# Two padding tiles change size: where the right-hand operands of TensorE start, modulo 512 bytes

## The chip, the cores and the metric

One core of one Trainium2 chip. The time is the device time of one execution in microseconds, the median of the runs shown; less is better. The profile was taken on one execution of the same program.

## What is computed

Attention through 32 pooled tokens per head, then two MLPs, all in float32 (only the sizes that matter are shown):

```
q, k, v: (8, 8, 576, 64)   p: (8, 8, 32, 64)
p_packed = softmax(p @ k.T / 8) @ v
a        = softmax(q @ p_packed.T / 8) @ p_packed      # -> x: (4608, 512)
x = (silu(x @ w_gate) * (x @ w_val)) @ w_out           # 512 -> 1536 -> 512
h = x @ w_in                                           # 512 -> 2048
return (h * cos(h)) @ w_out2                           # 2048 -> 512
```

## The kernel before, in words

Every large product is made with numbers split in two parts (`hi` and `lo`, type float32r): a product takes three matmuls, named by PASSES (hi·hi, hi·lo, lo·hi). Three of the four large products are, besides, done by a seven-product Strassen scheme; its seven products ("pieces") are numbered 0 to 6 and come in the order ORDER = 0, 4, 6, 1, 2, 3, 5. All work is issued in an order written out by hand, engine by engine; pools of tiles sit on the left or the right side of SBUF, and a pool's place is fixed by what is open on its side.

The stages, with their TensorE lines:

- **First MLP, gate and value products with attention** (L535, and L495 for their weights): per batch and per 128 hidden columns, matmuls of 288 moving columns. Moving operand `a2`, stationary operand `wp`, both in the pool `ups` on the right.
- **First down projection** (L652, function `strassen`): five sets of tokens, four with 512 moving columns per matmul and one, the fourth, with 256. Seven pieces of 36 matmuls in each set. Moving operand `g` (pools `da`, `db`, on the left), stationary operand `w1`. The tiles of `w1` lie on the left for pieces 0, 3 and 5 and on the right, in the pool `gates`, for pieces 4, 6, 1 and 2:

```
575     W1_AT = {0: ("da", 3), 3: ("db", 6), 5: ("db", 6)}
...
583             both = late["gates"].tile([128, 2, 2, 512], F32R, tag="w", name="w1", bufs=6)
...
652                         PE.matmul(
653                             out=acc[:, m, :N], lhsT=wd1[n, fp][:, j, 256 * x + 128 * m:256 * x + 128 * m + 128],
654                             rhs=g1[n, fp][:, y, j, :],
```

- **Second MLP, up projection** (L971, function `product`): 2016 matmuls of 384 columns, moving operand `xs`, stationary operand `up`:

```
971                 PE.matmul(
972                     out=out, lhsT=w[:, u, 128 * k:128 * k + 128], rhs=x[:, v, k, :],
```

- **Second MLP, down projection** (L1056, function `down_mm`): 2016 matmuls of 384 columns, moving operand `xs` (new tiles of the same pool), stationary operand `wd`.

`up` and `wd` lie on the left. `xs` has a pool of its own on the right, opened once `gates` and `pad` are closed, near the end of the first down projection. ScalarE and VectorE write `xs` and `g` in a helper (L111, L112).

Two tiles are never read or written; they only shift what comes after them on the right side: `right_pad` in the pool `pad` (opened first, so that it shifts `gates` and `ups`) and `late_pad` in the pool of `xs`:

```
101     ident = pad.tile([128, 128], F32, name="ident")
102     zero = pad.tile([128, 128], F32, name="zero")
103     pt = [pad.tile([128, NPAIR, NP], F32, name=f"pt{i}") for i in range(2)]
104     pad.tile([128, 8], F32, name="right_pad")
...
900                     late["x"] = ctx.enter_context(tc.tile_pool(name="xs", bufs=1, side="right", reuse_waits="tile"))
901                     x_now = [new_xs() for _ in range(7)]
902                     late["x"].tile([128, 8], F32, name="late_pad")
```

Of the kernel before, what the change touches and what calls it, by code (L numbers as in the profile page):

```python
# [10 lines left out]
F32 = mybir.dt.float32  # L11
# [55 lines left out]
def attention_mlp_kernel(ctx: ExitStack, tc: tile.TileContext, qT, kT, vP, pP, wgv, w12, out):  # L67
# [6 lines left out]
    def pool(n, side=None):  # L74
        kw = {"side": side} if side else {}
        return stage[n].enter_context(tc.tile_pool(name=n, bufs=1, reuse_waits="tile", **kw))

    pad = pool("pad", "right")
# [22 lines left out]
    ident = pad.tile([128, 128], F32, name="ident")  # L101
    zero = pad.tile([128, 128], F32, name="zero")
    pt = [pad.tile([128, NPAIR, NP], F32, name=f"pt{i}") for i in range(2)]
    pad.tile([128, 8], F32, name="right_pad")
    half_pi = cst.tile([128, 1], F32, name="half_pi")
    quarter = cst.tile([128, 1], F32, name="quarter")
    warm = cst.tile([128, 1], F32, name="warm")
# [348 lines left out]
    def w2_flush():  # L456
        while w2_dve:
            w2_dve.pop(0)()

    def w2_step():  # L460
        w2_flush()
        if w2_todo:
            w2_dve.append(w2_todo.pop(0)())
# [133 lines left out]
    def load_h(s_, k, t):  # L597
        if s_ < len(SETS):
            t0, N = SETS[s_]
            for fp in range(3):  # L600
                r = raw1[s_, k, t, fp] = hr_tile((k, t), [128, 2, N], "hr")
                f0 = NP1 * k + 2 * fp
                SP.dma_start(out=r, in_=h1[f0:f0 + 2, :, t0 + N * t:t0 + N * t + N].rearrange("f p n -> p f n"))
# [10 lines left out]
    def prep(s_, n, fp):  # L614
        if s_ >= len(SETS):
            return
        N = SETS[s_][1]
        k, t = {0: (0, 0), 4: (1, 0), 6: (1, 1), 1: (1, 1), 3: (0, 1), 2: (0, 0), 5: (1, 0)}[n]
        g = g1[n, fp] = g_first.pop() if g_first else new_g(N)
        split(raw1[s_, k, t, fp], g[:, 0], g[:, 1])  # L620

    def sums1(s_, i):
        todo = {
            1: [((0, 1), (0, 1), (0, 0), fp) for fp in range(3)],
            2: [((1, 1), (1, 1), (0, 1), fp) for fp in range(3)],
            3: [((0, 0), (1, 1), (0, 0), fp) for fp in range(3)],
            4: [((1, 0), (1, 0), (1, 1), 0)],
            5: [((1, 0), (1, 0), (1, 1), fp) for fp in (1, 2)],
        }
        for to, x, y, fp in todo.get(i, ()):  # L630
            to, x, y = (raw1[s_, k, t, fp] for k, t in (to, x, y))
            DVE.tensor_tensor(out=to, in0=x, in1=y, op=ALU.subtract)
# [55 lines left out]
    late = {}  # L688
# [16 lines left out]
    def load_x2(c):  # L705
        for a in range(2):
            for t in range(2):
                xb[a, t] = xt([128, 2, TH], F32, "xb")
                r0 = 2 * TH * c + TH * t
                SP.dma_start(out=xb[a, t], in_=x2d[2 * a:2 * a + 2, :, r0:r0 + TH].rearrange("k p n -> p k n"))  # L710
# [7 lines left out]
    def sums_x2(n):  # L718
        sum_x2(*(("t1", (0, 1), (0, 0)), ("t2", (1, 1), "t1"), ("t3", (1, 1), (0, 1)), ("t4", (1, 0), "t2"))[n])
        if n == 2:  # L720
            del xb[0, 1]

    def new_xs():
        return late["x"].tile([128, 2, 2, TH], F32R, tag="xs", name="xs", bufs=9)

    def split_x2(n, to):
        if to[n] is None:
            to[n] = new_xs()
        split(xb.pop(RIGHT[n]), to[n][:, 0], to[n][:, 1])

    with tc.manual_schedule():
# [142 lines left out]
        def nxt(s_, i):  # L874
            return (s_, ORDER[i + 1]) if i < 6 else (s_ + 1, ORDER[0])

        for s_ in range(len(SETS)):
            end = s_ == len(SETS) - 1
            for i in range(7):
                evict = strassen(s_, i)  # L880
                sums1(s_, i)
                for fp in range(3):
                    prep(*nxt(s_, i), fp)
                if i == 4:
                    load_h(s_ + 1, 0, 0)
                elif i == 5:
                    load_h(s_ + 1, 1, 1)
                    load_h(s_ + 1, 0, 1)
                elif i == 6:
                    load_h(s_ + 1, 1, 0)  # L890
                for _ in range(STEPS_D[s_][i]):
                    w2_step()
                if (s_, i) == (3, 6):
                    w2_flush()
                if end and i == 1:
                    load_x2(0)
                elif end and i == 4:
                    stage["gates"].close()
                    stage["pad"].close()
                    late["x"] = ctx.enter_context(tc.tile_pool(name="xs", bufs=1, side="right", reuse_waits="tile"))  # L900
                    x_now = [new_xs() for _ in range(7)]
                    late["x"].tile([128, 8], F32, name="late_pad")
                    for n in range(3):
                        sums_x2(n)
                elif end and i == 5:
                    sums_x2(3)
                elif end and i == 6:
                    for n in range(7):
                        split_x2(n, x_now)
                evict()  # L910
# [396 lines left out]
```

## Time and profile before

| | us |
|---|---|
| runs | 1423.08, 1420.67, 1418.03 |
| median | 1420.67 |
| the profiled execution | 1422.05 |
| its span in the profile | 1420.3 |

The profiled execution has 1.7 us outside its span and is 1.4 us above the median. The profile's times are microseconds of the span; a group of instructions has a count, a busy time and the mean length of one. Matmuls are pipelined: one starts before the last has ended, so the length of a matmul (393 ns, say) is not what it costs. What it costs is the distance from its start to the next one's start. The timeline gives a merged group of matmuls with its start, its length from the first start to the last end, and its count; the distance is (length less one matmul's length) divided by (count less one). All distances below are worked out so.

### The profile page before, as it was taken

The page shows a single profiled execution, that of the slowest core. Times are in us where ns is not written, and L with a number is a line of the kernel's source. Part 1 is how long each engine was busy: PE and PEld are TensorE (multiplying, and loading weights), DVE is VectorE, ACT ScalarE, POOL GpSimd, SP SyncE. Part 2 cuts the span into 40 slices and gives each one's busy share as a digit, 9 for nine tenths or more (in the row PEclk, how much of TensorE's full clock was granted, in tenths as well). Part 3 has the DMA queues.
Part 4 walks back from the last instruction along what each step waited for, and adds up shares of the span by engine and source line. Part 5 has one row for each costly group of instructions (what it writes and reads, how often), then busy time and mean ns, then how long its engine had stood idle before and what let it go on. Part 6 is the DMA issues. An engine that isn't in the chain of part 4 may idle for free.

```text
span 1420.3 us, 25277 instructions
## 1 busy us (share of the span) xinstructions
PE 1400.6 (99%) x9644; PEld 1286.9 (91%) x9644; DVE 1132.3 (80%) x1515; ACT 829.2 (58%) x1226; POOL 258.6 (18%) x424
## 2 busy tenths in 40 slices
PE   8999999999999999999999999999999999999998
PEld 6678888888898888897899999999999999999998
DVE  6779889888857898997768778787778778787785
ACT  5856666656645555553567777686775444444442
POOL 1112222222220111121011111121211202112020
PEclk9999999999999999999999999999999999999999
DMA  8947978786898746556584233242897765747641
GB/s 343 408 164 275 352 273 301 286 320 249 290 365 315 262 153 245 183 198 242 194 343 155 111 147 144 112 149 108 290 382 243 270 203 188 245 134 262 209 130 34
DMA packets 148504, 329.35 MB, mean 232 GB/s; under 512 B 21664, under 2 KB 58016, under 8 KB 146976
## 3 DMA queue, kind: packets, MB, share of 16 engines
q1 hardware_dynamic: 111040, 202.15, 40.7%
q0 software_dynamic: 36480, 123.76, 22.4%
q10 hardware_dynamic: 864, 1.84, 0.4%
q8 instruction: 76, 1.25, 0.4%
q14 instruction: 44, 0.36, 0.1%
HBM read 202.38 MB, written 125.30 MB: 231 GB/s over the span
## 4 chain that ended last, share of the span: by engine, by line
PE 73%; issue 13%; DVE 5%; DMA 4%; POOL 3%; ACT 2%; SPq 0%; POOLq 0%; DVEq 0%; ACTq 0%
PE o L652 16%; PE o L1056 15%; PE pv L535 7%; PE pg L535 7%; PE ac L971 7%; PE pb L1056 4%; PE pd L1056 4%; PE pd L971 3%; POOL h L991 2%; PE wp L495 2%; PE pb L971 2%; PE pv L524 2%; PE pg L524 1%; DMA hr<-h 1%; PE pp L234 1%
## 5 line engine op out<-in xcount | busy, mean ns | idle before, releaser
L652 PE MATMUL o<-g,w 128*128 128x512 f32 (+1 forms) x1260 | 263.6, 371 | 3.5 <-DVE g L112 1.8
L652 PEld LDWEIGHTS o<-g,w 128*128 128x128 f32 x1260 | 218.8, 188 | 47.9 <-DVE g L112 2.8
L1056 PE MATMUL o<-xs,wd 128*128 128x384 f32 x1440 | 254.3, 336 | 0.5 <-DVE xs L112 0.5
L1056 PEld LDWEIGHTS o<-xs,wd 128*128 128x128 f32 x1440 | 251.9, 187 | 0.9 <-DVE xs L112 0.9
L971 PE MATMUL ac<-xs,up 128*128 128x384 f32 x1152 | 219.5, 338 | 0.6 <-ACT v L1008 0.6
L971 PEld LDWEIGHTS ac<-xs,up 128*128 128x128 f32 x1152 | 204.5, 187 | 1.0 <-ACT v L1008 0.9
L112 DVE TENSOR_TENSOR xs<-raw,xs 128x768 fp32r<-128x768 f32 x168 | 149.6, 950 | 36.1 <-ACT xs L111 36.1
L111 ACT ACTIVATE xs<-raw 128x768 fp32r<-128x768 f32 x168 | 132.4, 843 | 73.1 <-DVE raw L1095 70.8
L111 ACT ACTIVATE g<-hr 128x1024 fp32r<-128x1024 f32 (+1 forms) x105 | 101.1, 975 | 91.8 <-PE o L652 42.3
L535 PE MATMUL pv<-a,wp 128*128 128x288 f32 x1008 | 150.6, 298 | 2.9 <-DVE h L567 2.8
L535 PEld LDWEIGHTS pg<-a,wp 128*128 128x128 f32 x1008 | 137.7, 188 | 16.8 <-issue 5.7
L535 PE MATMUL pg<-a,wp 128*128 128x288 f32 x1008 | 150.3, 298 | 0.5 <-ACT E L208 0.5
L535 PEld LDWEIGHTS pv<-a,wp 128*128 128x128 f32 x1008 | 137.6, 188 | 11.5 <-DVE h L567 5.7
L112 DVE TENSOR_TENSOR g<-hr,g 128x1024 fp32r<-128x1024 f32 (+1 forms) x105 | 113.1, 1113 | 35.5 <-ACT g L111 35.2
L553 ACT ACTIVATE silu<-pg 128x576 f32<-128x576 f32 x96 | 62.4, 651 | 112.8 <-PE pg L535 103.9
L971 PE MATMUL pd<-xs,up 128*128 128x384 f32 x576 | 117.2, 338 | 0.0
L567 DVE TENSOR_TENSOR h<-silu,pv 128x576 f32<-128x576 f32 x96 | 72.1, 751 | 52.2 <-PE pv L535 17.2
L971 PEld LDWEIGHTS pd<-xs,up 128*128 128x128 f32 x576 | 102.8, 187 | 0.0
L568 POOL DMA_DIRECT2D h<-h x96 | 53.4, 556 | 243.6 <-DVE h L567 221.7
L1105 POOL DMA_DIRECT2D out<-ot x80 | 49.5, 622 | 243.7 <-DVE ot L1100 181.5
L1095 DVE TENSOR_TENSOR raw<-raw,raw 128x768 f32<-128x768 f32 x96 | 85.3, 948 | 3.0 <-DMA raw<-h 3.0
L1011 DVE TENSOR_TENSOR hs<-v,pd 128x384 f32<-128x384 f32 x96 | 53.0, 552 | 33.7 <-PE pd L971 29.7
(130 smaller groups left out, 2065.6 us busy)
## 6 DMA issues: line engine op xcount, KB each, us to landing
raw<-h SPq DMA_DIRECT2D x96, 384.0 KB, 7.6
wd<-w2d SPq DMA_DIRECT2D x136, 256.0 KB, 4.0
h<-h POOLq DMA_DIRECT2D x96, 288.0 KB, 5.4
hr<-h SPq DMA_DIRECT2D x48, 512.0 KB, 7.5
raw<-in_w SPq DMA_DIRECT2D x44, 512.0 KB, 5.0
h<-cp POOLq DMA_DIRECT2D x48, 384.0 KB, 2.9
h<-cs POOLq DMA_DIRECT2D x48, 384.0 KB, 2.8
up<-w2u SPq DMA_DIRECT2D x56, 256.0 KB, 6.4
```

The costliest lines, as they stand in the source:

```text
L111: ACT.activation(out=hi, in_=src, func=AF.Copy)
L112: eng.tensor_tensor(out=lo, in0=src, in1=hi.bitcast(F32), op=ALU.subtract)
L535: PE.matmul(out=p_[:, c, :HS], lhsT=w[:, u, x, o:o + 128], rhs=a2[b][:, u, y, HS * c:HS * c + HS], start=(n == 0), stop=(n == 5),)
L553: ACT.activation(out=s_, in_=pg[:, :, :HS], func=AF.Silu)
L567: DVE.tensor_tensor(out=h_, in0=s_, in1=pv[:, :, :HS], op=ALU.mult)
L568: nc.gpsimd.dma_start(out=h1[f, :, S * b:S * b + S], in_=h_.rearrange("p c n -> p (c n)"))
L652: PE.matmul(out=acc[:, m, :N], lhsT=wd1[n, fp][:, j, 256 * x + 128 * m:256 * x + 128 * m + 128], rhs=g1[n, fp][:, y, j, :], start=(first a ...
L971: PE.matmul(out=out, lhsT=w[:, u, 128 * k:128 * k + 128], rhs=x[:, v, k, :], start=(first and k == 0 and i == 0), stop=(k == 1 and i == 2) ...
L1011: DVE.tensor_tensor(out=out, in0=x, in1=y, op=ALU.add)
L1056: PE.matmul(out=acc[m], lhsT=wd[n, 2 * fp + j][:, x, 128 * m:128 * m + 128], rhs=g2[n, fp][:, y, j, :], start=(first and fp + j + q == 0), ...
L1095: DVE.tensor_tensor(out=to, in0=x, in1=y, op=ALU.subtract)
L1105: eng.dma_start(out=out[r0:r0 + TH, c0:c0 + 64].rearrange("(b r) d -> r b d", r=32), in_=ot[32 * al:32 * al + 32].rearrange("p b m c -> p ...
```

## The change

```diff
@@ -101,7 +101,7 @@
     ident = pad.tile([128, 128], F32, name="ident")
     zero = pad.tile([128, 128], F32, name="zero")
     pt = [pad.tile([128, NPAIR, NP], F32, name=f"pt{i}") for i in range(2)]
-    pad.tile([128, 8], F32, name="right_pad")
+    pad.tile([128, 24], F32, name="right_pad")
@@ -899,7 +899,7 @@
                     x_now = [new_xs() for _ in range(7)]
-                    late["x"].tile([128, 8], F32, name="late_pad")
+                    late["x"].tile([128, 128], F32, name="late_pad")
```

`right_pad` grows by 64 bytes per partition, `late_pad` by 480. Nothing else differs: on every engine the same instructions stand in the same order. The first moves every tile of `pad`, `gates` and `ups` down by 64 bytes, the second moves `xs` down by 480. Start addresses in a partition, modulo 512 bytes, as the two programs allot them (all slices that TensorE takes of `g`, `w1`, `xs`, `up`, `wd` and `wp` are whole multiples of 512 bytes apart, so that one number holds for all of them):

| product | moving operand, before and now | stationary operand, before and now |
|---|---|---|
| first MLP (L535) | `a2` 64, 192, 320, 448; now 0, 128, 256, 384 | `wp` 320; now 256 |
| first down, pieces 0, 3, 5 (L652) | `g` 256; the same | `w1` 256; the same |
| first down, pieces 4, 6, 1, 2 (L652) | `g` 256; the same | `w1` 320; now 256 |
| second MLP, up and down (L971, L1056) | `xs` 448; now 480 | `up`, `wd` 256; the same |

## Rows read from the trace of the kernel before

**Rows 1.** The page's first two parts: busy time by engine, TensorE's granted clock.

```profile
PE 1400.6 (99%) x9644; PEld 1286.9 (91%) x9644; DVE 1132.3 (80%) x1515; ACT 829.2 (58%) x1226; POOL 258.6 (18%) x424
...
PEclk9999999999999999999999999999999999999999
```

**Rows 2.** Groups of TensorE, shapes kept apart: busy us, mean ns | idle before.

```profile
L1056 PE MATMUL o<-xs,wd 128*128 128x384 f32 x1440 | 254.3, 336 | 0.5 <-DVE xs L112 0.5
L652 PE MATMUL o<-g,w 128*128 128x512 f32 x1008 | 233.6, 393 | 2.8 <-ACT g L111 1.7 <-DVE g L112 1.1
L535 PE MATMUL pg<-a,wp 128*128 128x288 f32 x1008 | 150.3, 298 | 0.5 <-ACT E L208 0.5
L652 PE MATMUL o<-g,w 128*128 128x256 f32 x252 | 30.3, 282 | 0.7 <-DVE g L112 0.7
```

**Rows 3.** Timeline, L652 of 512 columns: start us, length us, group, count.

```profile
443.75 33.53 PE L652 MATMUL o<-g,w 128*128 128x512 f32 x143
477.81 23.53 PE L652 MATMUL o<-g,w 128*128 128x512 f32 x103
501.63 33.76 PE L652 MATMUL o<-g,w 128*128 128x512 f32 x144
535.69 23.53 PE L652 MATMUL o<-g,w 128*128 128x512 f32 x103
```

**Rows 4.** Timeline, L652 of 256 columns (the fourth set).

```profile
610.02 4.24 PE L652 MATMUL o<-g,w 128*128 128x256 f32 x34
614.22 4.05 PE L652 MATMUL o<-g,w 128*128 128x256 f32 x33
624.80 3.00 PE L652 MATMUL o<-g,w 128*128 128x256 f32 x25
```

**Rows 5.** Timeline, second MLP: two stretches of the up projection, four of the down.

```profile
1051.71 1.22 PE L971 MATMUL pb<-xs,up 128*128 128x384 f32 x6
1052.77 1.22 PE L971 MATMUL pd<-xs,up 128*128 128x384 f32 x6
...
1067.79 17.48 PE L1056 MATMUL o<-xs,wd 128*128 128x384 f32 x98
...
1086.51 5.81 PE L1056 MATMUL o<-xs,wd 128*128 128x384 f32 x32 [0.54 <-DVE xs L112]
...
1086.79 7.44 PE L1056 MATMUL o<-xs,wd 128*128 128x384 f32 x42
...
1299.77 30.03 PE L1056 MATMUL o<-xs,wd 128*128 128x384 f32 x171
```

**Rows 6.** Timeline, first MLP: matmuls of 288 columns in dozens.

```profile
340.45 1.85 PE L535 MATMUL pg<-a,wp 128*128 128x288 f32 x12
342.14 1.76 PE L535 MATMUL pv<-a,wp 128*128 128x288 f32 x12
343.73 1.76 PE L535 MATMUL pg<-a,wp 128*128 128x288 f32 x12
345.33 1.25 PE L224 MATMUL tp<-ident,E 128*128 128x128 f32 x10
```

**Rows 7.** TensorE's largest waits: us in total, times, longest us.

```profile
PE pv L535 <- DVE h L567: 2.8, 5, 1.4
PE o L652 <- DVE g L112: 1.8, 3, 0.8
PE o L652 <- ACT g L111: 1.7, 1, 1.7
```

**Rows 8.** Chain of waits in order of time, 630 to 651 us; engine table, two stretches.

```profile
630.02 6.28 DMA w2d<-w2p
...
637.82 13.22 DMA hr<-h
...
561.00:593.00 32.00, 32.00 (x139) 25.79 (x138) 1.00 0.32 114
632.30:640.30 8.00, 8.00 (x69) 8.00 (x68) 1.00 1.02 367
```

**Rows 9.** Groups on VectorE: the writer of `xs`, and a like one not moved.

```profile
L112 DVE TENSOR_TENSOR xs<-raw,xs 128x768 fp32r<-128x768 f32 x168 | 149.6, 950 | 36.1 <-ACT xs L111 36.1
L1095 DVE TENSOR_TENSOR raw<-raw,raw 128x768 f32<-128x768 f32 x96 | 85.3, 948 | 3.0 <-DMA raw<-h 3.0
```

## The prediction

> **What bounds the kernel now.** I read the page's busy times first: TensorE is busy 99% of the span at a granted clock of nine tenths or more in every slice, the 2.4 GHz level [rows 1]. Then its waits: the three largest come to 6.3 us of 1420 [rows 7]. So the kernel ends when TensorE has got through its 9644 matmuls, and since the change neither adds nor moves an instruction, it can act on the time only through the distance between two matmuls' starts, or through those few waits. That distance is read from the timeline: a group's length, less one matmul's mean length [rows 2], over its count less one.
>
> In the first down projection with 512 columns the reader is to see two speeds that alternate with the pieces [rows 3]: (33.53 - 0.393) / 142 = 233.4 ns and 33.37 / 143 = 233.3 ns in pieces 4, 6, 1, 2; (23.53 - 0.393) / 102 = 226.8 ns, twice, in pieces 3, 5 and the following 0. The clock and the shape are the same. By the table of start addresses, what differs is the weights: 320 modulo 512 in the slow pieces, 256 in the quick ones. The kernel before thus holds, for this part, both the old and the new state.
>
> With 256 columns [rows 4] the order is reversed: weights at 256 take (4.24 - 0.282) / 33 = 119.9 ns; at 320 they take 3.77 / 32 = 117.8 ns, and after a wait 2.72 / 24 = 113.3 ns. The two "all at 256" values fix a line: 226.8 - 119.9 = 106.9 ns for 256 more columns, 0.418 ns a column, and a fixed part of 226.8 - 213.8 = 13.0 ns. On it 384 columns cost 173.4 ns and 288 cost 133.3.
>
> The second MLP, whose tokens start at 448 and weights at 256, has three speeds at the same addresses [rows 5]: 1.06 us for six, or 176.7 ns, through the up projection (its groups of six start 1.06 us apart) and on to 1085 us, (17.48 - 0.336) / 97 = 176.7; after a wait of 0.54 us, (7.44 - 0.336) / 41 = 173.3; and from about 1096 us to the end 29.69 / 170 = 174.7. A wait can shift the stream of matmuls into another rhythm, and the slowest two lie 3.3 and 1.3 ns above the line, the middle one on it. The first MLP runs at 1.59 and 1.60 us for twelve, 132.5 to 133.3 ns: on the line or just under it [rows 6].
>
> **The change, part by part.** *Weights of the first down projection from 320 to 256.* Four sets have 4 slow pieces of 36 matmuls: 576 x (233.3 - 226.8 = 6.5 to 6.6 ns) = 3.8 us less. The fourth set pays: 72 x 2.1 + 72 x 6.6 ns = 0.6 us more. Sum -3.2 us, from the same code and shape on both sides. What could take it back is a wait: TensorE waits some 3.5 us around 623 and 651 us [rows 7], where the chain runs through a transfer of `hr` that takes 13.22 us, with the DMA engines full (1.02) at 632 to 640 us [rows 8]. Before that, at 561 to 593, they are at 0.32, so the transfers there come when TensorE's progress frees their buffers, and they move up with it. I take nothing off; if the landing did not move at all, the 2.8 us gained in the three sets ahead would go (bound).
>
> *Tokens of the second MLP from 448 to 480.* No row shows 480. The nearest rows are those of the same matmuls at 448: 173.3, 174.7 and 176.7 ns. Further off is the first down projection with its 19.5 ns of fixed part (233.3 - 213.8), which would be 179.9 ns for 384 columns; and its quickest, 113.3 with 256 columns, 6.6 below the line, would be 166.8. I take 173.4, on the line: it is the steady price of two of the four address pairs that rows show apart, this very shape ran at it for 7 us, and the first MLP's mixture of addresses lies within 1 ns of it. I hold the 176.7 and 174.7 for rhythms that 448 falls into and the line for what is left when the stream isn't thrown out of step; that 480 avoids them is my choice, not a reading. Then: 2016 matmuls of the up projection and some 150 of the down (1058 to 1086 us) save 3.3 ns, 7.1 us; some 1855 (1096 to 1420 us at 174.7) save 1.3, 2.4 us. Sum -9.5 us. Bounds: at 166.8, -36 us, held unlikely since no 512- or 384-column row has less than 13 ns of fixed part; at 179.9, +17 us.
>
> *First MLP.* Tokens and weights move by the same 64 bytes, so their spacing stays, and the speed is on the line already: nothing. Bounds for its 2016 matmuls: 6.2 ns less (the quickest row's 6.6 under the line: 126.7), -12.5 us; 6.9 more (19.5 ns of fixed part), +14 us.
>
> *VectorE, ScalarE, transfers.* The writer of `xs` takes 950 ns at 448 and a like subtraction on tiles that do not move takes 948 [rows 9]; if 480 cost it anything, it would lie beside TensorE, since VectorE is busy 80% [rows 1] and the largest group that reads `xs` idled 0.5 us before it in all [rows 2]. Nothing.
>
> **Sum:** -3.2 - 9.5 = -12.7 us on the profiled execution, 1422.05 to 1409.3. That execution was 1.4 us above the median, so the median goes from 1420.67 to **1408**.
>
> **What the skill says.** Rows 3 show 6.6 ns a matmul that go with the weights' address. The Trainium skill (TensorE: Matmul & The Clock Gate, Part 2, step by step) says that TensorE reads weights and streamed operand through two independent ports, so that loading the next weights takes nothing from the running matmul. Taken strictly, addresses would not matter and the sum would be 0; the row speaks against it unless the two kinds of piece differ by something else (second rival). The same skill (SBUF — State Buffer, Specifications) gives SBUF 16-byte lines; 448 and 480 are both whole multiples of 16, so by it `xs` would gain nothing: that is the first rival's second half.
>
> **The rivals.**
> 1. *Only the first down projection gains* (0.17). 480 falls into the same rhythms as 448. For: three speeds at one address show that the address doesn't decide alone. Against: in the first down projection 64 bytes did decide, every time. 1420.67 - 3.2 = 1417.5; by rhythm alone the second MLP could add 3.7 us (all at 176.7) or take 7.1 (up at 173.4).
> 2. *Nothing gains* (0.08). The slow pieces' weights lie on the right side, the quick ones' on the left; the far side, not the 64 bytes, would be the cause, and no pad changes the side. For: the rows cannot part the two. Against: the up projection, with weights on the left and tokens on the right, isn't at the slow value either. 1420.7.
> 3. *Slower* (0.20). 480 is no multiple of 64, and every other start in the table of before is. If the stream of 1536 bytes then touches one more piece of memory a matmul and meets the weight load twice, the fixed part goes to the 19.5 ns of the slow pieces: 179.9 ns. Price: 2166 x 3.2 + 1855 x 5.2 + 42 x 6.6 ns = 16.9 us, less 3.2: +13.7, 1434. It decides as soon as the distance passes about 176.6 ns on average, for there it eats the 3.2 us. For: the slow value exists, 64 bytes away from a quick one. Against: it appears at one spacing of tokens and weights alone (64 bytes), which 480 against 256 is not.
> 4. *More than the forecast* (0.10). The first MLP too falls to a quicker rhythm, half or all of 12.5 us: 1396 to 1402.
>
> **How the numbers follow.** My forecast has 0.45, its own range 1404 to 1412 (a rhythm may hold in part of a stage, and the 2.8 us of wait may come back). About 0.3%, 4.3 us, is what a measurement of this kernel can tell from no change. Faster: forecast and rival 4, 0.55. Same: rivals 1 and 2, 0.25. Slower: rival 3, 0.20. The range 1396 to 1430 takes in rivals 4, 1 and 2 and the lower half of 3; it leaves out the rest of 3 and the far bounds.
>
> **What would show it.** Right: every 512-column stretch of the first down projection at 226.8 ns, all 256-column ones at 119.9, six matmuls of the up projection 1.04 us apart, the down projection at 173.4 ns, the first MLP still at 1.59 to 1.60 us for twelve, and TensorE's waits near 650 us no longer than now. Wrong: 233 ns still in pieces 4, 6, 1, 2 (rival 2), 1.05 to 1.06 us for six (rival 1), 1.08 (rival 3), or waits that grow by what the matmuls give.

## The result and the profile after

The changed kernel takes 1407.85 us (median of 4 runs, 1407.60 to 1409.73) against 1421.00 us before (4 runs beside it): a ratio of 0.9904, 95% interval 0.9885 to 0.9924, so 13 us or 1% faster. The profiled execution has a span of 1406.1 us.

The page's busy times answer to [rows 1]: TensorE still fills 99% of the span, with 13 us less.

```profile
PE 1387.7 (99%) x9644; PEld 1277.7 (91%) x9644; DVE 1130.1 (80%) x1515; ACT 828.4 (59%) x1226; POOL 258.0 (18%) x424
...
PEclk9999999999999999999999999999999999999999
```

Where the stages begin and end shows where the time went. The instructions of one line, with first and last start (us); first the kernel before:

```profile
L535 PE MATMUL pg<-a,wp x1008: 288/295/511, 89.7 to 433.8; 128*128 128x288 f32 x168
...
L652 PE MATMUL o<-g,w x1260: 276/389/502, 435.6 to 702.3; 128*128 128x512 f32 x144, 128*128 128x256 f32 x36
...
L971 PE MATMUL ac<-xs,up x1152: 338/338/447, 702.5 to 1064.3; 128*128 128x384 f32 x192
```

and the changed kernel:

```profile
L535 PE MATMUL pg<-a,wp x1008: 288/295/509, 90.0 to 434.1; 128*128 128x288 f32 x168
...
L652 PE MATMUL o<-g,w x1260: 277/389/505, 435.9 to 696.9; 128*128 128x512 f32 x144, 128*128 128x256 f32 x36
...
L971 PE MATMUL ac<-xs,up x1152: 333/336/444, 697.1 to 1052.2; 128*128 128x384 f32 x192
```

| stage, from first start to the next stage's | before | after | difference |
|---|---|---|---|
| up to the first MLP | 89.7 | 90.0 | +0.3 |
| first MLP (L535) | 345.9 | 345.9 | 0 |
| first down projection (L652) | 266.9 | 261.2 | -5.7 |
| second MLP, to the end of the span | 717.8 | 709.0 | -8.8 |

The timeline of the changed kernel answers to [rows 3, 4, 6]: start, length, group, count.

```profile
443.81 33.48 PE L652 MATMUL o<-g,w 128*128 128x512 f32 x147
...
501.16 32.12 PE L652 MATMUL o<-g,w 128*128 128x512 f32 x141
...
611.79 3.88 PE L652 MATMUL o<-g,w 128*128 128x256 f32 x31
...
625.75 4.00 PE L652 MATMUL o<-g,w 128*128 128x256 f32 x32
...
342.43 1.76 PE L535 MATMUL pv<-a,wp 128*128 128x288 f32 x12
344.02 1.76 PE L535 MATMUL pg<-a,wp 128*128 128x288 f32 x12
345.62 0.60 PE L224 MATMUL tp<-ident,E 128*128 128x128 f32 x4
```

Worked out as before: (33.48 - 0.389) / 146 = 226.7 ns and 31.73 / 140 = 226.7 where the slow pieces 4, 6, 1, 2 had 233.3; (3.88 - 0.283) / 30 = 119.9 and (4.00 - 0.283) / 31 = 119.9 where the fourth set had 117.8 and 113.3; and 1.59 and 1.60 us for a dozen in the first MLP, as before.

For the second MLP two long windows give the distance: window over (count less 2), since a matmul of 336 ns that began before the window is counted too. Columns: stretch, its length, TensorE busy (count), granted clock, share of the DMA engines, GB/s. Up projection and down projection, before:

```profile
720.00:1040.00 320.00, 320.00 (x1813) 1.00 0.46 174
1120.00:1400.00 280.00, 280.00 (x1605) 1.00 0.55 182
```

and changed:

```profile
720.00:1040.00 320.00, 320.00 (x1847) 1.00 0.48 181
1120.00:1400.00 280.00, 279.76 (x1615) 1.00 0.54 179
```

That is 176.7 and 174.7 ns before; now 320 / 1845 = 173.4, and in the down projection, where the window reaches 0.24 us past the last matmul, 279.76 / 1613 = 173.4. The waits answer to [rows 7]:

```profile
PE o L652 <- DVE g L112: 1.4, 2, 0.8
PE o L1056 <- DVE xs L112: 1.2, 1, 1.2
...
PE o L652 <- ACT g L111: 0.3, 1, 0.3
```

### The profile page after: what moved, and what is told of

It is laid out like the page before. It is cut to its first block, busy times and chain, and to the rows that moved or that the text cites. A ratio compares the mean times of both kernels' runs of the same rounds, so it can differ in the third digit from the quotient of the medians.

```text
span 1406.1 us, 25277 instructions
## 1 busy us (share of the span) xinstructions
PE 1387.7 (99%) x9644; PEld 1277.7 (91%) x9644; DVE 1130.1 (80%) x1515; ACT 828.4 (59%) x1226; POOL 258.0 (18%) x424
## 4 chain that ended last, share of the span: by engine, by line
PE 74%; issue 13%; DVE 5%; POOL 3%; DMA 2%; ACT 2%; POOLq 0%; DVEq 0%; ACTq 0%
PE o L652 17%; PE o L1056 15%; PE pv L535 7%; PE pg L535 7%; PE ac L971 7%; PE pb L1056 4%; PE pd L1056 4%; PE pd L971 3%; PE wp L495 3%; POOL h L991 3%; PE pb L971 2%; PE pv L524 2%; PE pg L524 1%; DMA hr<-h 1%; PE pp L234 1%
## 5 line engine op out<-in xcount | busy, mean ns | idle before, releaser
L652 PE MATMUL o<-g,w 128*128 128x512 f32 (+1 forms) x1260 | 259.7, 368 | 1.7 <-DVE g L112 1.4
L652 PEld LDWEIGHTS o<-g,w 128*128 128x128 f32 x1260 | 219.3, 189 | 41.8 <-DVE g L112 1.9
L1056 PE MATMUL o<-xs,wd 128*128 128x384 f32 x1440 | 252.2, 336 | 1.2 <-DVE xs L112 1.2
L1056 PEld LDWEIGHTS o<-xs,wd 128*128 128x128 f32 x1440 | 249.8, 188 | 1.5 <-DVE xs L112 1.5
L971 PE MATMUL ac<-xs,up 128*128 128x384 f32 x1152 | 215.9, 336 | 0.6 <-ACT v L1008 0.6
L971 PEld LDWEIGHTS ac<-xs,up 128*128 128x128 f32 x1152 | 201.1, 188 | 1.0 <-ACT v L1008 0.9
L535 PE MATMUL pv<-a,wp 128*128 128x288 f32 x1008 | 150.6, 298 | 2.9 <-DVE h L567 2.7
L535 PEld LDWEIGHTS pg<-a,wp 128*128 128x128 f32 x1008 | 137.7, 188 | 16.8 <-issue 5.7
L535 PE MATMUL pg<-a,wp 128*128 128x288 f32 x1008 | 150.3, 298 | 0.4 <-ACT E L208 0.4
L535 PEld LDWEIGHTS pv<-a,wp 128*128 128x128 f32 x1008 | 137.6, 188 | 11.4 <-DVE h L567 5.7
L971 PE MATMUL pd<-xs,up 128*128 128x384 f32 x576 | 115.5, 336 | 0.0
L971 PEld LDWEIGHTS pd<-xs,up 128*128 128x128 f32 x576 | 101.0, 188 | 0.2
L997 DVE SCALAR_TENSOR_TENSOR cp<-ac,cp 128x768 f32<-128x768 f32 x48 | 45.9, 955 | 40.4 <-ACT cp L994 40.0
```

The source lines that it names most:

```text
L535: PE.matmul(out=p_[:, c, :HS], lhsT=w[:, u, x, o:o + 128], rhs=a2[b][:, u, y, HS * c:HS * c + HS], start=(n == 0), stop=(n == 5),)
L652: PE.matmul(out=acc[:, m, :N], lhsT=wd1[n, fp][:, j, 256 * x + 128 * m:256 * x + 128 * m + 128], rhs=g1[n, fp][:, y, j, :], start=(first a ...
L971: PE.matmul(out=out, lhsT=w[:, u, 128 * k:128 * k + 128], rhs=x[:, v, k, :], start=(first and k == 0 and i == 0), stop=(k == 1 and i == 2) ...
L997: DVE.scalar_tensor_tensor(out=out, in0=h_, scalar=1.0 / TWO_PI, in1=out.bitcast(I32), op0=ALU.mult, op1=ALU.subtract)
L1056: PE.matmul(out=acc[m], lhsT=wd[n, 2 * fp + j][:, x, 128 * m:128 * m + 128], rhs=g2[n, fp][:, y, j, :], start=(first and fp + j + q == 0), ...
```

## The experiments

Two questions were open. Do the two pads act apart, or does the second MLP's rhythm depend on how it is entered? And is it the start of the tokens alone that counts (480 good, 448 bad), or the **spacing**, the tokens' start less the weights' start? All edits below are against the changed kernel.

**1. The first pad alone, 2. the second pad alone.**

```diff
-                    late["x"].tile([128, 128], F32, name="late_pad")
+                    late["x"].tile([128, 8], F32, name="late_pad")
```

> The first pad alone (right_pad 24, late_pad 8): weights of the first down projection at 256, tokens of the second MLP back at 448. My theory (the two pads act apart, each on its own product): 226.8 ns in all 512-column pieces, the second MLP at 176.7 or 174.7 ns in most of its length, time 1415 to 1418. Rival (the second MLP's rhythm is set by when and how it is entered, and the first pad set it right): 173.3 ns in the second MLP although its tokens start at 448, time near 1408.

```diff
-    pad.tile([128, 24], F32, name="right_pad")
+    pad.tile([128, 8], F32, name="right_pad")
```

> The second pad alone (right_pad 8, late_pad 128): tokens of the second MLP at 480, first down projection as before. My theory: pieces 4, 6, 1, 2 at 233.3 ns again, second MLP at 173.3 ns, time 1411 to 1413. Rival (entry sets the rhythm): the second MLP at 174.7 or 176.7 ns in part, time 1416 to 1421.

The first pad alone: 1419.19 us (10 runs, 1414.78 to 1424.03), ratio 0.9985 (0.9966 to 1.0004), not told from no change and some 1 to 4 us over what I expected. The second alone: 1414.09 (6 runs, 1412.51 to 1418.24), ratio 0.9955 (0.9936 to 0.9973), 1 us above my numbers. In the first, L652 is quick and the second MLP slow in both windows:

```profile
443.71 33.48 PE L652 MATMUL o<-g,w 128*128 128x512 f32 x147
```

```profile
720.00:1040.00 320.00, 320.00 (x1814) 1.00 0.46 174
1120.00:1400.00 280.00, 280.00 (x1586) 1.00 0.55 182
```

The down projection is at 280 / 1584 = 176.8 ns here, 2 ns worse than in the profile of before, at the same addresses: so what the first pad gave was spent in this execution (its time, 1423.58, is one of the slowest of the ten). In the second, L652 is slow and the second MLP quick:

```profile
443.68 33.51 PE L652 MATMUL o<-g,w 128*128 128x512 f32 x143
```

```profile
720.00:1040.00 320.00, 320.00 (x1848) 1.00 0.48 182
1120.00:1400.00 280.00, 280.00 (x1617) 1.00 0.55 181
```

By the distances each pad acts on its own product, and the entry is not what sets the second MLP right. The times alone would not show it: against the 1420.83 us of the kernel before beside them, the single pads gain 1.6 and 6.7 us, and both together 13. In both profiles a halved clock took part of the gain (last section): with the first pad alone the first down projection takes 263.6 us, where it takes 261.2 with both.

**3. Tokens at 480 with weights at 288, 4. tokens at 448 with weights at 224.** The first has the changed kernel's tokens and the old spacing, the second the old tokens and the changed kernel's spacing. In the first (in the second the pads are 120 and 8 floats, and `late_pad` is 8):

```diff
+        lt([128, 8], F32, "lp", "left_pad", 1)
         up = {}
         slots = [
...
         ]
+        lt([128, 120], F32, "lq", "left_rest", 1)
```

> Tokens of the second MLP at 480 as in the changed kernel, but up and wd moved from 256 to 288 by a pad on the left side, so that tokens stand 192 bytes above the weights as in the kernel before (448 above 256). Theory of spacing (the difference of the two starts modulo 512 decides): the rhythms of before come back, 174.7 to 176.7 ns in most of the second MLP, time 1411 to 1420. Theory of address (480 itself is the good start for tokens): 173.3 ns throughout, time near 1408.

> The mirror of the run before: tokens at 448 as in the kernel before, up and wd at 224, so that the spacing is the 224 bytes of the changed kernel (480 above 256). Theory of spacing: 173.3 ns throughout, time near 1408. Theory of address: 174.7 to 176.7 ns in most of the second MLP, time 1411 to 1420.

Tokens at 480, weights at 288: 1427.38 us, and the up projection is back at 320 / 1811 = 176.7 ns; the down projection runs at 173.4.

```profile
720.00:1040.00 320.00, 320.00 (x1813) 1.00 0.47 177
1120.00:1400.00 280.00, 280.00 (x1617) 1.00 0.58 193
```

Tokens at 448, weights at 224: 1419.57 us, 173.3 and 173.4 ns.

```profile
720.00:1040.00 320.00, 320.00 (x1848) 1.00 0.49 184
1120.00:1400.00 280.00, 280.00 (x1617) 1.00 0.55 183
```

So the spacing decides, and 480 has no virtue of its own. The total times were off by something neither theory had: the left pad shifts the first slots of `up` against the tiles they replace (the reason, as I read it), and TensorE waits for the first load, 8.7 us in the second and 8.1 in the first.

```profile
PE ac L973 <- DMA up<-w2u: 8.7, 1, 8.7
```

Less that wait, the times are 1419.3 and 1410.9. Behind it the granted clock is at 0.50, in the first as here:

```profile
708.00:712.00 4.00, 4.00 (x13) 0.50 1.05 396
```

There 17 starts in the first and 12 in the second lie 320 ns apart, some 2.4 and 1.8 us more.

**5. to 7. Tokens at 192, 256 and 0, weights at 256; 10. tokens at 320; 11. no second pad.** Only `late_pad` differs: 72, 56, 120, 40 floats, and none, as in

```diff
-                    late["x"].tile([128, 128], F32, name="late_pad")
+                    late["x"].tile([128, 72], F32, name="late_pad")
```

> Tokens of the second MLP at 192 (late_pad 72), weights at 256: tokens 64 bytes below the weights, the spacing of the slow pieces 4, 6, 1, 2 of the first down projection before (256 under 320). Theory of spacing, with the slow pieces' fixed part of 19.5 ns: 179.9 ns, time 1430 to 1436. Or, as those pieces did with 256 columns, a quick rhythm of 6.6 ns under the line: 166.8 ns, time 1380 to 1385. Theory of address (only the weights' own address, 256, counts): 173.3 ns, near 1408.

> Tokens of the second MLP at 256 (late_pad 56), the same as its weights: spacing 0, as in the quick pieces of the first down projection. Theory of spacing: 173.3 ns throughout, time near 1408, the same as the changed kernel with 480. Rival (480 alone is good): 174.7 to 176.7 ns, 1411 to 1420.

> Tokens of the second MLP at 0 (late_pad 120), weights at 256: spacing 256, one that no large product has alone. No theory names its value; if the spacings 192 and 448 are the bad ones and the rest give the line, 173.3 ns and time near 1408; if a quicker rhythm than the line exists for 384 columns, it would show here as less than 173 ns.

> Tokens of the second MLP at 320 (late_pad 40), weights at 256: spacing 64, the mirror of the slow spacing. Theory (192 modulo 256 alone disturbs): 173.3 ns throughout, time 1407 to 1411. Rival (any spacing of 64 bytes from a multiple of 256, above or below, disturbs): 176.7 or 174.7 ns in the up projection at least, time 1413 to 1420.

> The changed kernel without any late_pad: xs lies 512 bytes higher, at 480 modulo 512 again. If only the start modulo 512 (or a part of it) matters: 173.3 ns throughout, time 1407 to 1410, the same as the changed kernel. If the true address matters: 174.7 to 176.7 ns somewhere in the second MLP, time above 1411.

Tokens at 192 took 1415.64 us. None of my three numbers came: the up projection is at 176.7 ns, as with 448, and the down projection at 173.4. The spacing of the slow 512-column pieces disturbs 384 columns too, but not by the 6.5 ns that I carried over.

```profile
720.00:1040.00 320.00, 320.00 (x1813) 1.00 0.46 174
1120.00:1400.00 280.00, 280.00 (x1617) 1.00 0.55 181
```

Tokens at 256 took 1410.22, at 0 1408.87, at 320 1409.27 us, without a late pad 1409.29 (4 runs, 1408.06 to 1409.56; ratio 0.9898, 0.9867 to 0.9929). All four are undisturbed; tokens at 320, the last that I had doubts of, read

```profile
720.00:1040.00 320.00, 320.00 (x1848) 1.00 0.48 181
1120.00:1400.00 280.00, 280.00 (x1617) 1.00 0.55 180
```

The second MLP in these kernels (ns between starts; the up window, the down window; one profiled execution of each kernel, and one run each in 3 to 10):

| tokens, weights | spacing modulo 512 | modulo 256 | up | down |
|---|---|---|---|---|
| 448, 256 (before; first pad alone) | 192 | 192 | 176.7; 176.6 | 174.7; 176.8 |
| 480, 288 | 192 | 192 | 176.7 | 173.4 |
| 192, 256 | 448 | 192 | 176.7 | 173.4 |
| 480, 256 (changed; second pad alone; no late pad) | 224 | 224 | 173.4 or 173.3 | 173.3 to 173.4 |
| 448, 224 | 224 | 224 | 173.3 | 173.4 |
| 256, 256 and 0, 256 | 0 and 256 | 0 | 173.3 | 173.4 |
| 320, 256 | 64 | 64 | 173.3 | 173.4 |

The first down projection fits in: 256 under 320 is a spacing of 448, or 192 modulo 256, at 233.3 ns [rows 3]; there only the weights moved, so that its start and its spacing are not told apart. Of the spacings tried, 192 modulo 256 is the one that disturbs. Spacings of 32, 96, 128 and 160 were not tried in a product that has one spacing alone.

At 2.4 GHz (granted clock 1.00), columns plus 32 cycles would be 120.0, 133.3, 173.3 and 226.7 ns for 256, 288, 384 and 512 columns, and the undisturbed distances lie within 0.1 ns of that (for 288 columns, those of experiment 8 below). The disturbed 176.7 and 233.3 ns are the columns plus 40 and plus 48. This is arithmetic on the distances and gives no cause.

**8. and 9. The first MLP's spacing moved by 32 and by 64 bytes.**

```diff
+            ups.tile([128, 8], F32, name="ups_pad")
             wp0.append(ups.tile([128, 2, 2, 512], F32, tag="a2", name="wpp", bufs=2))
```

(16 floats in the second).

> The changed kernel with 32 bytes between wp and a2 in the first MLP: wp at 224, a2 still at 0, 128, 256, 384, so that the four spacings are 288, 416, 32, 160 in place of 256, 384, 0, 128. Theory of spacing: the first MLP's 132.7 ns changes, by up to 6 ns either way, 12 us at most, and nothing else does. Rival (the first MLP mixes four spacings and has no rhythm of its own): it stays within 0.5 ns, time 1407 to 1409.

> The changed kernel with 64 bytes between wp and a2 in the first MLP (wp at 192): its four spacings become 320, 448, 64, 192, so that half of the matmuls stand at 192 modulo 256, the value of all the slow stretches so far. If the theory (spacing 192 modulo 256 disturbs) holds for 288 columns too, the mean leaves the 132.7 to 133.3 ns seen so far: slower towards 139.8 (up to +14 us), or, as the 256-column pieces did at that spacing, quicker towards 126.7 (up to -12 us). If the mixture of spacings washes it out, 132.7 to 133.3 and time 1407 to 1410.

They took 1409.16 and 1409.79 us. At 32 bytes, a dozen takes 1.60 us each time, 133.3 ns, the value of the line for 288 columns:

```profile
343.10 1.76 PE L536 MATMUL pv<-a,wp 128*128 128x288 f32 x12
344.70 1.76 PE L536 MATMUL pg<-a,wp 128*128 128x288 f32 x12
346.30 0.93 PE L224 MATMUL tp<-ident,E 128*128 128x128 f32 x7
```

At 64 bytes it is 1.59 us, 132.5 ns:

```profile
341.82 1.75 PE L536 MATMUL pv<-a,wp 128*128 128x288 f32 x12
343.41 1.75 PE L536 MATMUL pg<-a,wp 128*128 128x288 f32 x12
345.00 1.26 PE L224 MATMUL tp<-ident,E 128*128 128x128 f32 x10
```

Here four spacings alternate within every dozen, and none of the mixtures is worth more than 1 ns a matmul: 2016 times 0.8 ns would be 1.6 us. The rival to my expectation (no rhythm of its own) came nearest. There is nothing to win here, and no kernel of the study is shown to beat the changed one; the one without a late pad does the same with 512 bytes less.

## Why the prediction was right

Forecast 1408 us; measured 1407.85. The mechanism held: in both products that the pads move, the distances came out as forecast. That the number came within 0.2 us is luck: the first down projection lost 2.5 us more than its term, the second MLP 0.7 less, and 0.3 were added ahead of both, so that the span fell by 14.2 us where the sum had 12.7, and the median by 13.2. Step by step:

- **First down projection, -3.2 us.** The distances came as read from the kernel before: 226.7 ns in all 512-column pieces (forecast 226.8), 119.9 in the 256-column ones. The stage lost 5.7 us, though. The step that was mis-sized is the wait: I bounded it between nothing and a loss of 2.8 us, and it shrank, from 3.5 us [rows 7] to 1.7. Another 0.7 us lies for the most part beside the same waits: summed from the single starts in the two traces, the starts around the waits come 4.8 us later than the steady distance before and 2.5 after, which is 2.3 us and not 1.8. What moved the wait was not isolated.
- **Second MLP, -9.5 us.** The choice that could not be read, 480 on the line at 173.4 ns, held to the digit in both windows, 6.7 us in the up projection alone. There is luck in it, as nothing that I had read favoured 480; but over weights at 256 the starts 0, 256 and 320 did as well, and only 448 and 192 did not. The line itself was drawn through two points of one spacing; 384 columns at four more spacings (173.3) and 288 in experiment 8 (133.3) have since come out on it. The stage lost 8.8: TensorE's largest wait for `xs` grew from 0.54 [rows 5] to 1.22 us. Why it grew is not shown: with the up projection as slow as before, experiments 3 and 5 waited 1.6 and 1.1 us. The counts of my sum were some 30 too many (2166, 1855 and 42 matmuls are 4063, and the stage has 4032), worth less than 0.1 us.
- **First MLP and VectorE, nothing.** 345.9 us before and after, and the writer of `xs` takes 949 ns where it took 950. That the spacing stays when both operands move by 64 bytes was the reason given, and experiments 3 and 4 show spacing to be the right notion in the second MLP.
- **Rival 1** (480 falls into the same rhythms) falls: 480 against 256 gave 173.3 to 173.4 ns in five kernels (experiments 8 and 9 have it too). Its reason, that one address shows several speeds, is true of spacing 192 modulo 256 alone.
- **Rival 2** (the far side of SBUF) falls: the same tiles on the right side run at 226.7 ns once they start at 256.
- **Rival 3** (slower) had the right kind of cause in the wrong place. I called the slow spacing "64 bytes", which is one of its two forms; the kernel before already sat on the other, 448 - 256 = 192. Its price was wrong too: at the slow pieces' own spacing, 384 columns cost 176.7 and 173.4 ns (experiment 5), not 179.9.
- **Rival 4** (the first MLP quicker) did not occur.

On the two rules weighed against the trace: rows 3, and experiments 3 and 4, show the matmuls' distance to hang on where weights and moving operand start with respect to each other. The Trainium skill (TensorE: Matmul & The Clock Gate, Part 2, step by step) has independent ports for the two, so that the next weight load takes nothing from the running matmul. At spacing 192 modulo 256 the matmul does pay something, 6.6 ns with 512 columns, though no run shows whether it pays it at a port. The skill's 16-byte lines (SBUF — State Buffer, Specifications) do not tell 448 from 480 either, and 3.3 ns lie between them. The measurements decide. What mechanism lies under the spacing stays open: no run looked at it, and the table above is all that is shown.

## What to carry to other kernels

Where TensorE is the bound and every matmul loads its weights, work out the distance between matmul starts stage by stage and compare it with the line through the best stages; a few ns over it, at full clock and without waits, can come from the starting addresses. Then look at moving start less stationary start: here a spacing of 192 modulo 256 bytes cost up to 6.6 ns a matmul, and a padding tile of a few dozen bytes took it away. It is no rule for every shape: with 256 columns that spacing was 2.1 to 6.6 ns quicker [rows 4], and in the first MLP's mixture it cost nothing (experiment 9). Put a pad where it does not shift other slots: the one on the left cost 8 us in a late load.

## What the runs showed that I had not expected

- **One spacing, several lasting speeds.** At 192 modulo 256 the 384-column stream holds 173.3, 174.7 or 176.7 ns for hundreds of us at a time. The two profiles at 448 over 256 differ by 2.1 ns in the down projection, which is 4 us over its 2016 matmuls. At every other spacing tried it was 173.3 to 173.4. The kernels with the disturbed second MLP also scatter more (before: 1418.80 to 1426.82 in 15 runs; changed: 1407.60 to 1409.73 in 4); that the speeds explain the scatter is argued, not shown. They cannot be all of it: with the second pad alone the second MLP is undisturbed, and its six runs still lie 5.7 us apart, the slowest at a mean granted clock of 0.995 and the two quickest at 0.999.
- **A wait that halves the clock, and the same wait that does not.** In the second experiment TensorE waits 2.09 us for `xs`, and then the granted clock drops to 0.50, the 1.2 GHz level:

```profile
1080.43 10.00 PE L1056 MATMUL o<-xs,wd 128*128 128x384 f32 x47 [2.09 <-DVE xs L112]
```

```profile
1082.00:1084.00 2.00, 2.00 (x8) 0.50 0.16 61
1084.00:1086.00 2.00, 2.00 (x10) 0.74 0.26 51
1086.00:1088.00 2.00, 2.00 (x13) 1.00 0.87 309
```

In the changed kernel the same 47 matmuls follow a wait of 1.22 us and take 8.43 us instead of 10.00:

```profile
1074.70 8.43 PE L1056 MATMUL o<-xs,wd 128*128 128x384 f32 x47 [1.22 <-DVE xs L112]
```

So the halved clock cost 1.6 us beside the wait. But the length of the wait alone does not decide. In experiment 10 the same matmuls follow a wait of 2.10 us at full clock:

```profile
1076.16 8.42 PE L1056 MATMUL o<-xs,wd 128*128 128x384 f32 x47 [2.10 <-DVE xs L112]
```

And with the first pad alone two waits of 0.96 and 0.76 us, near 648 us in the first down projection, halve it, while in the kernel before waits of 1.67 and 0.76 us in the same place left it at 1.00:

```profile
650.00:652.00 2.00, 2.00 (x7) 0.51 1.02 394
652.00:654.00 2.00, 2.00 (x8) 0.64 0.75 246
```

What decides is open. The wait for `xs` was 0.5 to 1.6 us in the kernels with a slow up projection and 1.2 to 2.1 us in the others. That a quicker TensorE makes it longer is thus likely but not isolated; it is the largest wait left in the second MLP.
